# The first pair's decay: a one-hot product on TensorE in place of a fetch from DRAM

## The chip, the cores and the metric

The kernel runs on one core of a Trainium2 chip. The metric is the device time of one execution in microseconds; the median of several executions is compared.

## What is computed

Attention with a cumulative decay over 4 batches, 8 heads, 576 positions and head size 64, then two gated layers over the 2304 tokens, all in 32-bit floats:

```
cum = cumsum(log(clip(f, 1e-4, 1)), axis=-1)             # [4, 8, 576]
scores = q @ k.T / sqrt(64) + cum[..., :, None] - cum[..., None, :]   # causal
attn = softmax(scores)
x = (attn @ v) as [2304, 512]
x = (sigmoid(x @ w_gate) * (x @ w_val)) @ w_out           # 512 -> 1536 -> 512
h = x @ w_in2
out = (h * clip(h + 3, 0, 6) / 6) @ w_out2                # 512 -> 2048 -> 512
```

In a row of scores `cum` at the query's own position is the same for every key, so the softmax needs only the term of the keys. The kernel keeps the scores negated and adds `cum` of the key.

## The kernel before

The attention works through 16 pairs of heads (class `Pair`, from line 293). For a pair the queries and keys of its two heads are loaded by SP (`load`, line 308; the values by `load_v`, line 314), turned by TensorE and copied to `qp` and `kp`, with a small piece for the last 64 queries in `qz` (`prep`, line 334). Then come four units of scores (`scores`, line 371): s=1 holds the first 256 queries, s=2 and s=3 the next two blocks of 128 (384 and 512 keys wide), and s=4 the last 64 queries of both heads together. For each unit VectorE adds the decay to the scores and takes the minimum of each row (`expo`, `least`, line 410), ScalarE (ACT in the profile) does the exponential with its sum, VectorE the reciprocal, GpSimd (POOL) the scaling (`norm`, line 456), TensorE turns the result (`flip`, tile `tt`), ScalarE copies it out, and TensorE multiplies it with the values (`values`, tile `pv`). SP issues nearly all loads and stores.

The decay that `least` reads is the tile `dc`: `cum` of the pair's two heads, 2 x 576 numbers, the same in all 128 partitions. At the start `cumulate` (line 268) loads f with (batch, head) on 32 partitions, clips it on VectorE, takes the logarithm on ScalarE, forms the running sum `cum` with one scan on VectorE and stores it to the DRAM tile `cum_d`. For each pair `load_decay` (line 317) fetches two rows of `cum_d` back, each spread over 128 partitions by the transfer. `tail_decay` (line 323) makes from `dc` a masked copy `dt` for s=4, on POOL. The pool of `dc` has two buffers, that of `dt` one.

The first pair is set up ahead of the loop, lines 1134 to 1140, and there stands `warm_up` too (line 1091): 24 products (`WU`) of a zero tile `z`, in bf16, 512 columns wide, whose results in the PSUM tiles `o` nobody reads. They write to the pool `psF` with two buffers, which later serves the products of the gated layer. The three-buffer pool `psB` holds the turned tiles `tq`, `tk`, `tl` and `tt`.

In the attention the order of the instructions on each engine is set by a scheduler, from its own estimate of times, except where `keep_in_program_order` binds TensorE's products. From the second layer on (line 1240) it is the order of the program. Between the attention's products TensorE gets pieces of the first gated layer (`Filler`), and VectorE, ScalarE and POOL convert that layer's weights (`single`, line 104; tile `raw`).

Of the kernel before, what the change touches and what calls it, by code (L numbers as in the profile page):

```python
# [7 lines left out]
F32 = mybir.dt.float32  # L8
# [4 lines left out]
ALU = mybir.AluOpType  # L13
# [7 lines left out]
def attn_moe_kernel(  # L21
# [13 lines left out]
    nc = tc.nc  # L35
    B, H, S, D = q.shape
# [3 lines left out]
    P = 128  # L40
# [3 lines left out]
    TAIL = S - NQ * P  # L44
# [15 lines left out]
    def split_sbuf(hi, lo, src, eng_hi, eng_lo):  # L60
# [10 lines left out]
        out=ident, in_=ident, compare_op=ALU.not_equal, fill=1.0, base=0,  # L71
        pattern=[[-1, P]], channel_multiplier=1,
# [6 lines left out]
    for d in (masks[:, :P], mask):  # L79
        nc.gpsimd.affine_select(  # L80
            out=d, in_=d, compare_op=ALU.is_ge, fill=BIG, base=0,
            pattern=[[-1, P]], channel_multiplier=1,
# [145 lines left out]
    pe = Tensor()  # L228
# [4 lines left out]
    a2 = att.enter_context(tc.tile_pool(name="a2", bufs=2))  # L233
# [3 lines left out]
    ep = att.enter_context(tc.tile_pool(name="ep", bufs=7))  # L237
    sm = att.enter_context(tc.tile_pool(name="sm", bufs=10))
    psA = att.enter_context(tc.tile_pool(name="psA", bufs=NA, space=PSUM))
    psB = att.enter_context(tc.tile_pool(name="psB", bufs=6 - NA, space=PSUM))  # L240
# [27 lines left out]
    def cumulate():  # L268

        fl = ax.tile([P, S], F32, tag="x0", name="fl")[: B * H]  # L270
        ones = ax.tile([P, S], F32, tag="x0", name="ones")[: B * H]
        cum = ep.tile([P, S], F32, tag="e", name="cum")[: B * H]
        nc.scalar.dma_start(fl, f.rearrange("b h s -> (b h) s"))
        nc.vector.memset(ones, 1.0)
        nc.vector.tensor_scalar(fl, fl, 1.0e-4, 1.0, ALU.max, ALU.min)
        nc.scalar.activation(fl, fl, AF.Ln)
        nc.vector.tensor_tensor_scan(cum, ones, fl, 0.0, ALU.mult, ALU.add)
        nc.scalar.dma_start(cum_d, cum)

    def load_nat(t, src, b, hp, last):  # L280

        for j in range(2):
            nc.sync.dma_start(
                t[:, :NQ, j, :], src[b, 2 * hp + j, : NQ * P, :].rearrange("(c p) d -> p c d", p=P)
            )
        for p0, x in last:
            nc.sync.dma_start(
                t[p0 : p0 + TAIL, NQ, :, :],
                x[b, 2 * hp : 2 * hp + 2, NQ * P : S, :].rearrange("h p d -> p h d"),
            )  # L290
        return t

    class Pair:
# [23 lines left out]
        def load_decay(self):  # L317
            h0 = self.b * H + 2 * self.hp
            self.dc = a2.tile([P, 2, S], F32, tag="dc", name="dc")
            both = cum_d[h0 : h0 + 2].rearrange("h s -> (h s)").rearrange("(o x) -> o x", o=1)  # L320
            nc.sync.dma_start(self.dc.rearrange("p h s -> p (h s)"), both.to_broadcast([P, 2 * S]))

        def tail_decay(self):


            self.dt = a1.tile([P, S], F32, tag="dt", name="dt")
            for j in range(2):
                r = slice(64 * j, 64 * j + 64)
                nc.gpsimd.affine_select(
                    out=self.dt[r], in_=self.dc[r, j], compare_op=ALU.is_ge, fill=BIG, base=NQ * P,  # L330
                    pattern=[[-1, S]], channel_multiplier=1,
                )
# [585 lines left out]
    class Second:  # L918
# [93 lines left out]
        def unit(self, k, x, ys, temps, between={}):  # L1012
            u1, u2, p5 = temps
            g, tt = self.ga[k % 2], nc.vector.tensor_tensor
            r11, r22, r12 = self.act(u1, g, 0, 0), self.act(p5, g, 1, 1), self.act(u2, g, 1, 0)
            r21 = self.act(x(), g, 0, 1)
            then = {1: (r11,), 2: (r11,), 3: (r11,), 4: (r22,), 5: (r12, r22, r22), 6: (r21, r12, r12, r21, r21)}
            for s in range(7):
                if s in (1, 3):
                    y = ys.pop(0)()  # L1020
                o = y if s % 2 else x()
                self.product(o, k, s, s in (0, 1, 3))
                if s in (0, 2, 3):
                    nc.scalar.copy({0: u1, 2: u2, 3: p5}[s], o)  # L1024
                elif s < 6:
                    c = {1: u1, 4: p5, 5: u2}[s]
                    tt(c, c, o, ALU.add)  # L1027
                for r in then.get(s, ()):
                    next(r)
                if k % NQ2 == NQ2 - 1:  # L1030
                    self.load_block(k // NQ2 * 7 + 7 + s)
                if s in between:
                    between[s]()
# [57 lines left out]
    def warm_up(n):  # L1091
        z = ep.tile([P, S], F32, tag="e", name="z").bitcast(BF16)[:, :512]
        nc.gpsimd.memset(z, 0.0)
        for _ in range(n):
            o = psF.tile([P, 512], F32, tag="F", name="o")
            nc.tensor.matmul(o, z[:, :P], z, start=True, stop=True)
# [6 lines left out]
    EA = (nc.scalar, nc.gpsimd, nc.gpsimd)  # L1103
    EF = (nc.scalar, nc.scalar, nc.gpsimd)
    WU = 24

    KD, TL = 4, 3

# [10 lines left out]
    psF = fa.enter_context(tc.tile_pool(name="psF", bufs=2, space=PSUM, side="right"))  # L1119
# [8 lines left out]
    fill = Filler(wa, NCA)  # L1128
    pairs = [
        Pair(i, i // NP, i % NP, list(range(1, NQ + 1) if i < UP else range(NQ, 0, -1)))  # L1130
        for i in range(B * NP)
    ]
    units = [(p, s) for p in pairs for s in p.order]
    cumulate()
    pairs[0].load()
    pairs[0].load_decay()
    pairs[0].load_v()
    pairs[0].tail_decay()
    warm_up(WU)
    pairs[0].prep()  # L1140
# [63 lines left out]
    for t in range(len(units) + 3):  # L1204
        for job in (scores, values, expo, flip, norm, some, prep):
            job(t)
        p, s = unit(t - 3)
        if p and s == p.order[-1] and p.hp == NP - 1 and p.b < NCA:
            done = p.b + 1
        p, s = unit(t - 5)  # L1210
# [71 lines left out]
```

## Time and profile before

| | us |
|---|---|
| three runs | 1030.00, 1032.05, 1037.42 |
| median | 1032.05 |
| profiled execution | 1031.56 |
| its span, first to last instruction | 1029.8 |

The profile shows one execution. Its engines are PE (TensorE's products) and PEld (TensorE's loads of the stationary operand), DVE (VectorE), ACT (ScalarE), POOL (GpSimd) and SP (the queue that issues DMAs, SPq). L215 is the helper through which the products go, L219 that of the transposes, so tiles tell them apart. A row of the timeline gives start, duration, engine, line, operation, output <- inputs, number of instructions and in brackets the idle time of the engine before it with what ended it. An f32 product that is not a transpose has two records for each instruction of the order, and consecutive ones overlap: what one costs the next is seen in the distance of their starts.

### The profile page before, as it was taken

The page shows a single profiled execution, that of the slowest core. Times are in us where ns is not written, and L with a number is a line of the kernel's source. Part 1 is how long each engine was busy: PE and PEld are TensorE (multiplying, and loading weights), DVE is VectorE, ACT ScalarE, POOL GpSimd, SP SyncE. Part 2 cuts the span into 40 slices and gives each one's busy share as a digit, 9 for nine tenths or more (in the row PEclk, how much of TensorE's full clock was granted, in tenths as well). Part 3 has the DMA queues.
Part 4 walks back from the last instruction along what each step waited for, and adds up shares of the span by engine and source line. Part 5 has one row for each costly group of instructions (what it writes and reads, how often), then busy time and mean ns, then how long its engine had stood idle before and what let it go on. Part 6 is the DMA issues. An engine that isn't in the chain of part 4 may idle for free.

```text
span 1029.8 us, 15579 instructions
## 1 busy us (share of the span) xinstructions
PE 1015.4 (99%) x5410; PEld 835.2 (81%) x5410; DVE 530.3 (51%) x1206; ACT 466.0 (45%) x1052; POOL 304.4 (30%) x385
## 2 busy tenths in 40 slices
PE   7999999999999999999999999999999999999998
PEld 4667766776778888998888888898988988989987
DVE  5687755536435654447568567444434444233222
ACT  5776466456554442323334434434434434334332
POOL 3576755445333322120324323111111111111110
PEclk9999999999999999999999999999999999999999
DMA  7987567355232435284696758766495755744211
GB/s 196 259 252 215 163 197 197 115 163 169 82 132 87 139 122 165 75 283 176 248 341 247 236 174 317 250 250 219 147 362 191 279 208 189 286 170 174 75 72 62
DMA packets 120911, 197.79 MB, mean 192 GB/s; under 512 B 63936, under 2 KB 73152, under 8 KB 116736
## 3 DMA queue, kind: packets, MB, share of 16 engines
q1 hardware_dynamic: 120736, 196.64, 57.0%
q8 instruction: 43, 0.70, 0.3%
q14 instruction: 36, 0.29, 0.1%
q10 hardware_dynamic: 96, 0.15, 0.0%
HBM read 143.47 MB, written 53.29 MB: 191 GB/s over the span
## 4 chain that ended last, share of the span: by engine, by line
PE 93%; DMA 2%; DVE 2%; ACT 1%; issue 1%; POOL 1%; SPq 0%; POOLq 0%; ACTq 0%; DVEq 0%
PE po L215 33%; PE pv L215 19%; PE u L215 17%; PE pg L215 15%; PE st L215 5%; PE tt L219 3%; DMA x_d<-x 1%; DMA big<-x_d 1%; PE tq L219 1%; PE tk L219 1%; DMA dc<-cum_d 0%; DVE e L411 0%; ACT e L419 0%; POOL e L456 0%; DVE raw L108 0%
## 5 line engine op out<-in xcount | busy, mean ns | idle before, releaser
L215 PE MATMUL po<-w,big 128*128 128x512 f32 x864 | 200.5, 390 | 0.0
L215 PEld LDWEIGHTS po<-w,big 128*128 128x128 f32 x864 | 161.9, 188 | 32.8
L215 PE MATMUL pg<-big,wg 128*128 128x512 f32 (+1 forms) x720 | 166.7, 373 | 2.6 <-DMA big<-x_d 2.6
L215 PE MATMUL pv<-big,wv 128*128 128x512 f32 (+1 forms) x720 | 166.7, 373 | 0.0
L215 PE MATMUL po<-big,wo 128*128 128x512 f32 (+1 forms) x720 | 164.4, 372 | 0.1
L215 PEld LDWEIGHTS po<-big,wo 128*128 128x128 f32 x720 | 124.9, 189 | 27.4 <-issue 2.9
L215 PEld LDWEIGHTS pg<-big,wg 128*128 128x128 f32 x720 | 124.2, 189 | 28.3 <-DMA big<-x_d 4.4
L215 PEld LDWEIGHTS pv<-big,wv 128*128 128x128 f32 x720 | 124.9, 189 | 24.7 <-issue 3.1
L1027 DVE TENSOR_TENSOR h<-h,u 128x384 f32<-128x384 f32 x69 | 38.2, 554 | 155.2 <-PE u L215 155.2
L456 POOL TENSOR_SCALAR e<-e,m 128x256 f32<-128x256 f32 (+4 forms) x144 | 85.2, 606 | 57.4 <-DVE m L454 35.1
L419 ACT ACTIVATE e<-e,m 128x256 f32<-128x256 f32 (+4 forms) x144 | 83.8, 584 | 39.2 <-DVE m L411 35.8
L215 PE MATMUL u<-h,big 128*128 128x384 f32 x504 | 90.6, 336 | 0.4 <-DVE h L1027 0.4
L215 PE MATMUL u<-h,h 128*128 128x384 f32 x504 | 90.2, 336 | 0.0
L215 PEld LDWEIGHTS u<-h,big 128*128 128x128 f32 x504 | 88.2, 188 | 2.1 <-DVE h L1027 1.1
L215 PEld LDWEIGHTS u<-h,h 128*128 128x128 f32 x504 | 88.4, 188 | 1.0
L976 POOL TENSOR_TENSOR big<-tail,big 128x384 fp32r<-128x384 f32 x30 | 30.8, 1027 | 196.3 <-PE u L215 115.7
L1024 ACT COPY h<-u 128x384 f32<-128x384 f32 x69 | 32.6, 473 | 112.9 <-PE u L215 112.9
L111 ACT ACTIVATE raw<-raw 128x512 f32<-128x512 f32 x68 | 45.5, 681 | 66.5 <-DVE raw L108 65.3
L739 DVE SCALAR_TENSOR_TENSOR sg<-sg,pv 128x512 f32<-128x512 f32 (+1 forms) x48 | 29.6, 618 | 82.8 <-PE pv L215 64.8
L411 DVE CUSTOM_DVE_ANT_0 e<-st,dc 128x384 f32<-128x384 f32 (+3 forms) x110 | 53.5, 519 | 32.5 <-PE st L215 27.1
L114 DVE SCALAR_TENSOR_TENSOR raw<-raw 128x512 int32<-128x512 int32 x68 | 52.1, 775 | 14.6 <-ACT raw L111 14.2
L219 PE MATMUL tt<-ident,e 128*128 128x128 f32 x384 | 55.8, 276 | 1.2 <-POOL e L456 1.2
(135 smaller groups left out, 1247.3 us busy)
## 6 DMA issues: line engine op xcount, KB each, us to landing
h<-xc_d SPq DMA_DIRECT2D x21, 768.0 KB, 6.8
big<-x_d SPq DMA_DIRECT2D x56, 256.0 KB, 3.6
raw<-in_moe_w_out_dram SPq DMA_DIRECT2D x28, 512.0 KB, 3.8
h<-wt_d SPq DMA_DIRECT2D x12, 1024.0 KB, 7.0
big<-wt_d SPq DMA_DIRECT2D x12, 1024.0 KB, 7.3
dc<-cum_d SPq DMA_DIRECT2D x16, 576.0 KB, 4.7
x_d<-x SPq DMA_DIRECT2D x32, 288.0 KB, 3.5
h<-wb_d SPq DMA_DIRECT2D x12, 768.0 KB, 4.5
```

The costliest lines, as they stand in the source:

```text
L111: nc.scalar.activation(e, e, AF.Copy, scale=2.0**-112)
L114: nc.vector.scalar_tensor_tensor(low, high, 3, low, ALU.logical_shift_left, ALU.bitwise_or)
L215: i = nc.tensor.matmul(*a, **k)
L219: i = nc.tensor.transpose(*a)
L411: i = nc.vector.tensor_tensor_reduce(out=e, in0=st, in1=d, op0=ALU.add, op1=ALU.min, scale=1.0, scalar=init, accum_out=m[:, a : a + 1],)
L419: nc.scalar.activation(e, e, AF.Exp, bias=m[:, a : a + 1], scale=-1.0, accum_out=m[:, 4 + b : 5 + b])
L456: nc.gpsimd.tensor_scalar(e, e, m[:, 12 + j : 13 + j], 1.0, ALU.mult, ALU.mult)
L739: pace["dve"] = nc.vector.scalar_tensor_tensor(sg, sg, 1.0, pv, ALU.add, ALU.mult)
L976: (nc.vector if f else nc.gpsimd).tensor_tensor(lo, sg, hi.bitcast(F32), ALU.subtract)
L1024: nc.scalar.copy({0: u1, 2: u2, 3: p5}[s], o)
L1027: tt(c, c, o, ALU.add)
```

## The change

`load_decay` is no longer called for the first pair. In its place `spread_decay` makes on POOL a tile `pick` of 32 partitions and 2 x 128 columns, which holds ones in the row of the first or of the second head and zeros elsewhere. Three pairs of f32 products on TensorE, each with `pick` of one head as the stationary and a stretch of `cum` as the moving operand (256, 64 and 256 columns), give `cum` of the head in all 128 partitions. ScalarE copies the first 256 and the last 64 columns of both heads from PSUM to `dc`, VectorE the middle 256. The first and the last stretch use `psF`, the tail `psB`. The store to `cum_d` stays, and all other pairs fetch as before.

```diff
@@ cumulate
         nc.scalar.dma_start(cum_d, cum)
+        return cum
@@ class Pair
+        def spread_decay(self, cum):
+
+            h0 = self.b * H + 2 * self.hp
+            pick = ep.tile([P, S], F32, tag="e", name="pick")[: B * H, : 2 * P].rearrange("p (j c) -> p j c", j=2)
+            nc.gpsimd.memset(pick, 0.0)
+            nc.gpsimd.affine_select(
+                out=pick, in_=pick, compare_op=ALU.not_equal, fill=1.0, base=-h0,
+                pattern=[[-1, 2], [0, P]], channel_multiplier=1,
+            )
+            self.dc = a2.tile([P, 2, S], F32, tag="dc", name="dc")
+            for c0, n, copy, pool, tag in (
+                (0, 2 * P, CO[0], psF, "F"), (4 * P, TAIL, CO[1], psB, "B"), (2 * P, 2 * P, CO[2], psF, "F")
+            ):
+                o = pool.tile([P, 512], F32, tag=tag, name="pd")[:, : 2 * n].rearrange("p (j c) -> p j c", j=2)
+                for j in range(2):
+                    pe.matmul(o[:, j], pick[:, j], cum[:, c0 : c0 + n], start=True, stop=True)
+                copy(self.dc[:, :, c0 : c0 + n], o)
@@
     WU = 24
+    CO = (nc.scalar.copy, nc.scalar.copy, nc.vector.tensor_copy)
@@
-    cumulate()
+    cum = cumulate()
     pairs[0].load()
-    pairs[0].load_decay()
     pairs[0].load_v()
+    pairs[0].spread_decay(cum)
     pairs[0].tail_decay()
     warm_up(WU)
```

The scheduler then puts the instructions of the first three pairs in another order; behind them every engine's order is the one before. On TensorE the start of the program was this (`identb` and `masks` for the causal mask, `qn` and `kn` the loaded q and k, `z` the warm-up):

```order
L215 MATMUL st<-masks,identb 128x384
L219 MATMUL tq<-ident,qn 128x128 x4
L1096 LDWEIGHTS z
L1096 MATMUL o<-z 128x512
L1096 LDWEIGHTS z
L1096 MATMUL o<-z 128x512
L219 MATMUL tk<-ident,kn 128x128 x4
```

and now, with `pd` the products with the one-hot tile, it is this:

```order
L215 MATMUL st<-masks,identb 128x384
L215 MATMUL pd<-cum,pick 128x256 x2
L215 MATMUL pd<-cum,pick 128x64 x2
L215 MATMUL pd<-cum,pick 128x256 x2
L219 MATMUL tq<-ident,qn 128x128 x4
L219 MATMUL tk<-ident,kn 128x128 x4
L1115 LDWEIGHTS z
L1115 MATMUL o<-z 128x512
L219 MATMUL tl<-ident,kn 128x128
```

The six products stand ahead of the first transposes, and no warm-up product stands ahead of either.

Further on, while the second pair's scores are made, TensorE's order before (tt_422 is the first turned tile of the first pair's s=3, tt_427 the second, tt_450 that of s=4; st_437 to st_485 are scores of the second pair) was:

```order
L1096 LDWEIGHTS z_192
L1096 MATMUL o_240<-z_192 128x512
L219 MATMUL tt_422<-ident_74,e_338 128x128 x4
L215 MATMUL st_437<-kp_313,qp_312 128x384
L215 MATMUL st_438<-kp_313,qp_312 128x384
...
L219 MATMUL tt_427<-ident_74,e_339 128x128 x4
L219 MATMUL tt_450<-ident_74,e_364 128x128 x4
```

and at the same place now (tt_438, tt_443 and tt_466 are the same three tiles):

```order
L219 MATMUL tt_438<-ident_74,e_354 128x128 x4
L1115 LDWEIGHTS z_208
L1115 MATMUL o_242<-z_208 128x512
L215 MATMUL st_453<-kp_329,qp_328 128x384
L215 MATMUL st_454<-kp_329,qp_328 128x384
...
L1115 LDWEIGHTS z_208
L1115 MATMUL o_244<-z_208 128x512
L219 MATMUL tt_443<-ident_74,e_355 128x128 x4
L1115 LDWEIGHTS z_208
L1115 MATMUL o_246<-z_208 128x512
L219 MATMUL tt_466<-ident_74,e_380 128x128 x4
```

The 24th warm-up product stood ahead of tt_422; now the 16th does, and eight follow, up to the values of the first pair.

On VectorE the order between the scan and the first score operation, which order prints as ISA, is now this:

```order
L277 SCALAR_TENSOR_TENSOR cum<-ones,fl 32x576
L340 COPY dc<-pd 128x2x256
L363 TENSOR_SCALAR qp<-tq 128x512
L368 COPY kp<-tk 128x512
L376 TENSOR_SCALAR qz_144<-tl 64x64 x2
L363 TENSOR_SCALAR qp<-tq 128x512
L430 ISA e,m<-st,dc 128x128
```

Before, it was the same without the copy. On SP the first pair's fetch of `dc` is gone; the third pair's, which stood between the loads of the fourth pair's k, now stands behind three loads of weights (`raw`) and right ahead of the fourth pair's own.

## Rows read from the trace of the kernel before

**Rows 1.** Page, busy us of each engine, share of the span, instructions.

```profile
PE 1015.4 (99%) x5410; PEld 835.2 (81%) x5410; DVE 530.3 (51%) x1206; ACT 466.0 (45%) x1052; POOL 304.4 (30%) x385
```

**Rows 2.** Windows: busy time by engine in each stretch, then granted clock, DMA share.

```profile
core 0: us, PE busy (x) PEld busy (x) DVE busy (x) ACT busy (x) POOL busy (x), PEclk, DMA share, GB/s
0.00:23.00 23.00, 17.65 (x93) 9.73 (x94) 12.92 (x50) 11.17 (x30) 8.97 (x25) 1.00 0.76 185
23.00:50.00 27.00, 26.84 (x185) 17.02 (x185) 17.92 (x73) 19.68 (x62) 13.84 (x24) 1.00 0.93 264
50.00:75.00 25.00, 23.84 (x165) 14.39 (x161) 20.27 (x67) 19.84 (x58) 19.34 (x27) 1.00 0.83 243
...
310.00:650.00 340.00, 340.00 (x1708) 290.56 (x1707) 201.52 (x313) 130.31 (x226) 89.53 (x68) 1.00 0.59 203
```

**Rows 3.** The chain that ended last, from its start: start us, us, what.

```profile
0.72 2.58 DMA fl<-in_f_dram
...
5.91 2.00 DMA cum_d<-cum
...
7.92 5.09 DMA dc<-cum_d
...
22.64 0.66 PE tt L219 x4
23.30 1.06 PE st L215 x6
```

**Rows 4.** Timeline of PE, 0 to 26 us.

```profile
4.29 1.09 PE L219 MATMUL tq<-ident,qn 128*128 128x128 f32 x4 [0.90 <-DMA qn<-in_q_dram]
5.17 1.06 PE L1096 MATMUL o<-z 128*128 128x512 bf16 x2
6.02 1.06 PE L219 MATMUL tk<-ident,kn 128*128 128x128 f32 x4
6.88 0.63 PE L1096 MATMUL o<-z 128*128 128x512 bf16 x1
...
10.21 0.63 PE L219 MATMUL tq<-ident,qn 128*128 128x128 f32 x4 [0.27 <-DMA qn<-in_q_dram]
10.68 1.90 PE L1096 MATMUL o<-z 128*128 128x512 bf16 x8
...
17.72 0.65 PE L215 MATMUL st<-kp,qz 128*128 128x288 f32 x2
18.21 0.59 PE L1096 MATMUL o<-z 128*128 128x512 bf16 x2
```

**Rows 5.** Timeline of all engines, 5 to 14 us: VectorE's operations and ACT's table load.

```profile
5.80 0.65 DVE L344 TENSOR_SCALAR qp<-tq 128x512 f32<-128x512 f32 x1
...
7.12 0.69 DVE L349 COPY kp<-tk 128x512 f32<-128x512 f32 x1 [0.67 <-PE tk L219]
...
7.99 1.28 ACT L419 ACT_TABLE_LOAD   x1
8.00 0.46 DVE L357 TENSOR_SCALAR qz<-tl 64x64 f32<-64x64 f32 x2 [0.19 <-ACT kp L354]
...
10.88 0.69 DVE L344 TENSOR_SCALAR qp<-tq 128x512 f32<-128x512 f32 x1 [2.41 <-PE tq L219]
...
13.03 0.29 DVE L411 CUSTOM_DVE_ANT_0 e<-st,dc 128x128 f32<-128x128 f32 x1 [1.47 <-DMA dc<-cum_d]
```

**Rows 6.** Waits of 22.6 to 31.3 us: waited for, us in total, times, longest.

```profile
DVE e L411 <- PE st L215: 2.1, 2, 1.1
```

**Rows 7.** Windows, the same stretch; columns as in the rows 2.

```profile
22.60:31.30 8.70, 8.66 (x65) 5.41 (x65) 6.04 (x27) 6.51 (x22) 4.31 (x9) 1.00 0.91 258
```

**Rows 8.** Timeline of SP and POOL, 28 to 33 us, and dc's transfer issued there.

```profile
28.18 0.41 SPq L321 DMA_DIRECT2D dc<-cum_d  x1
...
32.80 1.39 POOL L329 TENSOR_SCALAR_AFFINE_SELECT dt<-dc 64x576 f32<-64x576 f32 x2 [0.30 <-DVE m L411]
...
DMA to landing us min/median/max: 8.1/8.1/8.1
```

## The prediction

> **What bounds the kernel now.** I read the page's busy shares first: TensorE is busy for 1015.4 us of the 1029.8 us span [rows 1]. What is left is not spread evenly, and the windows show where it lies: the first 23 us hold 5.35 us of TensorE's idle time (23.00 - 17.65), the next 27 us hold 0.16 us, and from 310 to 650 us there is none [rows 2]. So two things set the time: when TensorE's queue fills up for good, and how much work it then holds. Next comes the chain that ended last, read from its start [rows 3]. It begins with the load of f, goes through clamp, logarithm and scan, whose result stands at 5.9 us, and then spends 2.00 us on the store to DRAM and 5.09 us on the fetch. VectorE's first score operation starts at 13.03 us, having waited 1.47 us for that fetch [rows 5]. From 22.64 us on the chain is TensorE, piece after piece.
>
> The profiled execution took 1031.56 us, 1.76 us more than its span and 0.49 us less than the median of 1032.05; the three runs reach from 1030.00 to 1037.42. My sum is made against 1031.56.
>
> **What goes.** The 7.1 us of store and fetch leave the chain. The store itself stays, since the other pairs need it, and one fetch of 576 KB less runs among the early loads. This does not buy 7.1 us. VectorE had nothing else to do only for the last 1.47 us: before that it stood in order behind the second pair's qp copy, which began at 10.88 and took 0.69 [rows 5]. If the decay were there at no cost and nothing else moved, the first score operation could start 1.47 us earlier, and that is the whole prize.
>
> **What comes: six products on TensorE, ahead of the transposes.** They wait for the scan, so they start at about 5.9 us, and the first transposes, which ran from 4.29 us before, now stand behind them. Their price: an f32 product over 288 columns, which is two passes and so two records, started at 17.72 and the next product at 18.21 [rows 4]; a pass takes 0.245 us, or 0.85 ns a column. The six have 1,152 columns, or 2,304 in two passes: 1.96 us. Early in this trace TensorE is slower than that. Two warm-up products take the 0.85 us from 5.17 to 6.02, 0.425 us each; eight of them from 10.68 take 1.90 us together, some 0.21 each [rows 4]. [...] At the early spacing, twice as long, the six take 3.9 us. Bounds: 2.0 and 3.9.
>
> [...]
>
> I take 3.9: TensorE began its transposes at 4.29 us before and still ran at the wide spacing up to 6.02 [rows 4]; now it starts 1.6 us later. So the products end at 9.8 us, and their last value is out 0.2 us after (the lone warm-up product at 6.88 lasts 0.63, against the spacing of 0.425 [rows 4]): 10.0 us.
>
> **Behind them, VectorE in order.** The order puts five VectorE operations between the products and the first score: the copy of the last third (128x512, as the kp copy, 0.69), qp 0.65, kp 0.69, the two qz pieces 0.46, and the second pair's qp 0.69 [rows 5]. That is 3.18 us, and the first score operation starts at 13.2 us, against 13.03. The transposes fit under it: after 9.8 us eight of them take 1.7 us even at the wide spacing of 0.215 each [rows 4], and qp needs only the first four. Two ACT copies lie beside the products. The load of the exp table (1.28 us [rows 5]) now starts behind the copy of kp's tail, at 11.3 to 12.4 us, and so ends at 12.6 to 13.7; the first exponential is due at about 13.5, so at worst it costs 0.2, which I leave out. POOL's two operations for the one-hot tile follow its memsets and end long before the scan does. So the start is +0.2 us late: the fetch's 7.1 us are given back to products and copies in front of the same operation. The bounds: at the fast spacing products end at 7.9 and VectorE's row would allow 11.3, but the second pair's q, for which TensorE waited until 10.21 [rows 4], holds its qp until about 11.6, so -1.4; if TensorE stays slow through the transposes, 13.9, so +0.9.
>
> **What moves: the warm-up products.** 24 stand in the program as before. Before, all had been issued when TensorE came to the first transposes of the 128x512 scores, at 22.64 us. Now eight of them stand behind that place, one or two between each group of transposes, scores and values. There they are not free: from 22.60 to 31.30 TensorE is busy for 8.66 of 8.70 us [rows 7], and VectorE waits there for TensorE's scores, 2.1 us in all, not the other way round [rows 6]. Eight at 0.216 (the spacing of the row of eight: 1.90 less the last one's 0.39, over seven) make 1.7 us. Bounds: nothing, if waits that only this order has leave room for them, and 1.7. I take 1.7, since the only rows of this place show no room.
>
> **SyncE.** With one fetch and its wait of 0.5 us gone, all loads behind go out about 1 us earlier; nothing waits for them in this stretch. One is put back: the third pair's decay, sent before at 22.2 us, now stands behind three weight loads, next to the fourth pair's. Its wait is met when the first pair's last score operation has read the buffer. POOL takes it at 32.80 us [rows 8]. I reckon it sent at 23 to 27 us, landed after 5 to 8 us, and not late: nothing.
>
> **Sum.** 1031.56 + 0.2 + 1.7 = 1033.5 us. A shift at 31 us goes through to the end: behind it the instructions stand in the order they had, and TensorE idles 1.2 us between 50 and 75 us and not at all from 310 to 650 [rows 2].
>
> **Rivals.**
> 1. *Faster: the products run at the fast spacing and the warm-up products fall in gaps.* The first score then starts at 11.6 us, 1.4 us early: 1031.56 - 1.4 = 1030.2. For it: the granted clock reads 1.00 throughout. Against it: the 0.425 us spacing, and the full TensorE behind 22.6 us. It decides if the last third is copied before about 9 us.
> 2. *The two terms cancel.* Either the fast products' 1.4 us pay for the eight (1031.56 - 1.4 + 1.7 = 1031.9), or the products are slow and the eight fit in gaps (1031.56 + 0.2 = 1031.8). For it: each bound by itself is possible; against: the same rows as above.
> 3. *Slower: the third pair's decay lands late.* The fetch sent at 28.18 us, behind the same three weight loads, took 8.1 us to land [rows 8]. Sent at 26.7 us it would land at 34.8, 2.0 us after POOL wanted it at 32.80; POOL's queue holds the scaling of the next probabilities behind that mask, and TensorE's transposes wait for those. With the slow start's 0.9: 1031.56 + 0.9 + 1.7 + 2.0 = 1036.2. It decides if the fetch lands after the place where POOL is ready for it. Against it: the loads run earlier, so it should be sent well ahead of that.
>
> **How the numbers follow.** Forecast 0.45, rival 1 0.15, rival 2 0.2, rival 3 0.2. The predicted time is the forecast's 1033.5. The range takes in all four, and stops a little outside their ends, at 1030.0 and 1036.6, for the spread of runs and what I can't see. A measurement of this kernel tells about 1%, 10 us, from no change. None of the cases comes near that: the whole prize is 1.47 us and the dearest rival costs 4.6. So within 1% has 0.93; 0.03 is left for faster and 0.04 for slower, for mechanisms that no row shows.
>
> **What would show it.** Right: in the profile after, the six products fill TensorE from 5.9 us to near 10; the first score operation on VectorE starts at 13.0 to 13.4 us and waits for VectorE's own queue, not for a DMA; from 22 to 32 us warm-up products stand among busy TensorE work and the second pair's values end about 1.9 us later than before. Wrong: a first score before 12 us; TensorE idle in front of the late warm-up products; or POOL waiting for the decay's DMA near 33 us. A gain or loss of more than 5 us would say that the order behind the start does more than carry a shift through.

## Result and the profile after

| | us |
|---|---|
| this kernel, median of 14 runs | 1037.65 (1035.54 to 1040.23) |
| kernel before, median of 14 runs beside it | 1031.64 (1030.00 to 1037.42) |
| ratio | 1.0053, 95% interval 1.0042 to 1.0064 |
| profiled execution after | 1040.23, span 1038.5 |

The change costs about half a per cent, 6.0 us by the medians. That is within 1%, as forecast, but it lies above the range. The profiled execution is the slowest of the 14; a second one (1035.24 us, below) is used beside it.

The page's busy row after, to be read against [rows 1]:

```profile
PE 1021.7 (98%) x5422; PEld 841.2 (81%) x5422; DVE 530.8 (51%) x1207; ACT 468.0 (45%) x1054; POOL 305.3 (29%) x387
```

TensorE is busy 6.3 us more and idle 2.4 us more (1038.5 - 1021.7 = 16.8 against 14.4). The chain that ended last begins like this after the change (start us, us, what), against [rows 3]:

```profile
4.70 1.36 DVE cum L277
...
6.19 4.60 PE pd L215 x12
10.79 1.05 PE tq L219 x4
11.84 0.85 PE tk L219 x4
...
13.75 0.53 PE tq L219 x4
...
14.50 0.91 PE st L215 x8
15.41 0.27 DVE e L430
```

From the scan to the first score operation everything is TensorE: the products, then the transposes with warm-up products between them, then the scores. VectorE's rows say the same; its operations wait for TensorE one after the other, and the first score operation starts at 15.39 us, not at 13.03 [rows 5]:

```profile
10.83 0.69 DVE L340 COPY dc<-pd 128x512 f32<-128x512 f32 x1 [4.78 <-PE pd L215]
11.87 0.69 DVE L363 TENSOR_SCALAR qp<-tq 128x512 f32<-128x512 f32 x1 [0.35 <-PE tq L219]
12.72 0.69 DVE L368 COPY kp<-tk 128x512 f32<-128x512 f32 x1 [0.16 <-PE tk L219]
...
14.33 0.69 DVE L363 TENSOR_SCALAR qp<-tq 128x512 f32<-128x512 f32 x1 [0.26 <-PE tq L219]
15.39 0.29 DVE L430 CUSTOM_DVE_ANT_0 e<-st,dc 128x128 f32<-128x128 f32 x1 [0.37 <-PE st L215]
```

Windows after (columns as in [rows 2]); the first three answer to [rows 2, 7]:

```profile
0.00:23.00 23.00, 17.26 (x81) 11.32 (x82) 12.67 (x41) 9.89 (x26) 7.19 (x23) 1.00 0.74 173
23.00:50.00 27.00, 26.93 (x186) 16.55 (x184) 16.27 (x69) 18.66 (x58) 13.74 (x24) 1.00 0.78 227
22.60:31.30 8.70, 8.70 (x54) 5.03 (x52) 4.28 (x23) 6.70 (x22) 5.30 (x10) 1.00 0.89 282
...
170.00:175.00 5.00, 4.45 (x20) 3.00 (x18) 1.63 (x5) 2.35 (x4) 2.17 (x4) 0.66 0.34 86
250.00:255.00 5.00, 3.54 (x13) 2.68 (x14) 3.06 (x11) 2.90 (x9) 2.60 (x6) 0.78 0.30 84
255.00:260.00 5.00, 5.00 (x39) 2.97 (x39) 2.98 (x12) 3.86 (x13) 2.79 (x4) 0.88 0.08 20
```

In the first 23 us TensorE idles 5.74 us, hardly more than the 5.35 before. So the 4.60 us of products did not go into its waits; they stand in front of its work. The last three rows are new: here the granted clock is 0.66, 0.78 and 0.88. The trace's list of granted clocks has 0.50 from 170.83 and from 252.75 us, 3.41 us each time, and 1.00 between them and behind, up to 1037.82. Before, it was 1.00 in the same stretches:

```profile
170.00:175.00 5.00, 5.00 (x33) 3.73 (x30) 2.78 (x6) 1.70 (x5) 3.28 (x6) 1.00 0.85 223
250.00:255.00 5.00, 5.00 (x28) 3.73 (x29) 2.88 (x5) 1.37 (x3) 2.89 (x5) 1.00 0.86 255
```

What the clock lost is 5 x 0.34 = 1.7 us in the first place and 5 x (0.22 + 0.12) = 1.7 us in the second.

Ahead of both places TensorE waits. Its timeline after (the first row, sixteen products of the gated layer, is a mark that stood at 140.85 us before):

```profile
144.51 3.95 PE L215 MATMUL po<-big,wo 128*128 128x512 f32 x16
...
169.12 0.73 PE L215 MATMUL pg<-big,wg 128*128 128x512 f32 x2 [1.85 <-DMA big<-x_d]
169.69 0.60 PE L219 MATMUL tq<-ident,qn 128*128 128x128 f32 x4
170.84 2.08 PE L215 MATMUL pg<-big,wg 128*128 128x512 f32 x4 [0.55 <-DMA big<-x_d]
...
251.40 0.73 PE L215 MATMUL pg<-big,wg 128*128 128x512 f32 x2 [2.26 <-DMA big<-x_d]
```

At the turn from one batch to the next the attention's x is stored to DRAM (`x_d<-x`) and loaded again (`big<-x_d`) for the gated products. Before, the waits for it were 0.80 and 1.41 us (and 0.35 a little later). The same rows before:

```profile
140.85 3.95 PE L215 MATMUL po<-big,wo 128*128 128x512 f32 x16
...
164.41 0.73 PE L215 MATMUL pg<-big,wg 128*128 128x512 f32 x2 [0.80 <-DMA big<-x_d]
...
243.46 0.73 PE L215 MATMUL pg<-big,wg 128*128 128x512 f32 x2 [1.41 <-DMA big<-x_d]
```

The shift was 3.66 us at the mark and still so at 163 us, 7.10 behind the first reload, 9.20 behind the second and 8.7 at the end. Of the two steps, 3.44 and 2.10 us, the longer waits make 1.60 and 0.50 (1.85 + 0.55 - 0.80; 2.26 - 1.41 - 0.35); the rest, 1.8 and 1.6, agrees with the two falls of the clock. So the loss has two parts: one from the start, one from the two reloads.

### The profile page after: what moved, and what is told of

Read it like the earlier page. It is cut to its first block, busy times and chain, and to the rows that moved or that the text cites. A ratio compares the mean times of both kernels' runs of the same rounds, so it can differ in the third digit from the quotient of the medians.

```text
span 1038.5 us, 15608 instructions
## 1 busy us (share of the span) xinstructions
PE 1021.7 (98%) x5422; PEld 841.2 (81%) x5422; DVE 530.8 (51%) x1207; ACT 468.0 (45%) x1054; POOL 305.3 (29%) x387
## 4 chain that ended last, share of the span: by engine, by line
PE 94%; DVE 2%; DMA 2%; ACT 1%; issue 1%; POOL 0%; SPq 0%; POOLq 0%; ACTq 0%; DVEq 0%
PE po L215 33%; PE pv L215 18%; PE u L215 17%; PE pg L215 15%; PE st L215 6%; PE tt L219 3%; DMA x_d<-x 1%; PE tk L219 1%; PE tq L219 1%; DMA big<-x_d 1%; PE pd L215 0%; PE o L1115 0%; DVE e L430 0%; ACT e L438 0%; DVE raw L108 0%
```

## Experiments

They are numbered as their labels. In all of them the kernel before ran beside on the same chip; its medians were 1029.9 to 1031.1 us. A "mark" is the first of the sixteen products above, at 140.85 us in the profile before and 144.51 after.

**1 and 2: are the late warm-up products dear?** The changed kernel with 16 and with none:

```diff
-    WU = 24
+    WU = 16        # second: WU = 0
```

> The changed kernel with 16 warm-up products in place of 24: TensorE's order is the same but for the last eight, which are gone. Theory A (the late start and the eight warm-up products among busy work make the loss): the eight stand in the chain that ended last between 26 and 33 us, so it takes 8 x 0.216 = 1.7 us less than the changed kernel's 1037.65, about 1035.9, and the third pair's first 128x384 scores come 1.7 us earlier than 39.66 us. Rival B (the eight lie in gaps, the loss is made at the start and in later DMA waits): no less than 1037.2. Rival C (the loss is made by the waits on the reload of x near 165 and 250 us): no change in the place of the third pair, and a time that follows those waits.

> The changed kernel without any warm-up product. Theory A: the chain between 18.8 and 33 us holds some 15 of them, so up to 3.2 us less than 1037.65, about 1034.5, if TensorE still comes to its fast spacing as early as it does now (14 us). Rival (the warm-up products are what brings the fast spacing early): transposes and scores stay at twice the spacing beyond 14 us, the first score starts no earlier than 15.4 us, and the time is 1037 or more.

With 16: 1037.77 us, ratio 1.0067 (1.0046 to 1.0088); first score 15.32, mark 144.26. Taking away the eight late ones moved the mark by 0.25 us and the time not at all. Its chain shows what takes their place, a wait for VectorE:

```profile
27.15 0.46 PE tt L219 x4
27.60 0.41 issue
28.02 0.56 DVE e L430
```

The reading by which they cost 0.216 us each falls; they lie in gaps that this order has. With none: 1034.39 us, 1.0037 (1.0023 to 1.005); first score 14.94, mark 144.31. The mark did not move, yet 3.4 us went. In the profiles the difference lies behind the mark: with 16 the wait near 245 us was 2.58 us with a clock of 0.74 behind it, with none 1.31 us and no fall.

**3: the kernel before without warm-up.**

```diff
-    WU = 24
+    WU = 0
```

> The kernel before without any warm-up product, decay fetched as before. Theory A: the first score waits for the fetch at 13.0 us whatever TensorE does, and the warm-up products lay in waits, so 1031 to 1032, as before. Rival (they bring the fast spacing early and their loss costs): 1033 or more, with twice the spacing beyond 13 us.

1031.64 us, 1.0007 (0.9995 to 1.0019); first score 13.38. TensorE kept the wide spacing until 19 us (0.21 us a transpose from 15.86, 0.11 from 19.01) and the mark stood at 143.66, 2.8 us late, but the time hardly suffered: the waits for the reloads were 0.23 and 1.48 us.

**4: transposes ahead of the products, no warm-up.**

```diff
+    pairs[0].prep()
     pairs[0].spread_decay(cum)
     pairs[0].tail_decay()
-    warm_up(WU)
-    pairs[0].prep()
```

> The changed kernel with the first pair's transposes written ahead of the one-hot products, and no warm-up product. On TensorE the turned q and k come first, then the products. Theory A: the transposes run while the scan does, the products run from about 6.1 to 10.7 us at the wide spacing, and behind them only small copies are left, so the first score starts at 12.5 to 13.5 us, against 15.4; with no warm-up product in the chain the time is 1031 to 1033. Rival (the store and the late DMAs make the loss, not the start): 1036 or more though the first score is early.

1032.45 us, 1.0025 (1.0014 to 1.0035); products 3.71 and 1.04 us, first score 13.41, mark 143.53, waits 0.20 and 0.93. Two microseconds less than with none in the changed order: standing ahead of the transposes is what made the first score late.

**5: the changed kernel again, unaltered.**

> The changed kernel once more, unaltered, for a second profile of it. Theory (the start is late by 2.4 us for good, and on top the length of a store and reload of x varies from execution to execution; where TensorE waits about 2 us or more for one, its granted clock falls and the stretch behind costs 1.5 to 2 us more): first score 15.3 to 15.5 and +3.5 to +3.7 us at 141 us as in the first profile, but the waits for the reload at 165 and 250 us come out different from 1.85 and 2.26 us, and the executions with a mean clock of 0.999 to 1.0 lie within 1035 to 1037, those at 0.996 to 0.998 within 1037 to 1040. Rival (the new program makes these waits long by its order): both waits again within 0.3 us of 1.85 and 2.26, and the clock below 0.7 behind the first.

1036.08 us, 1.0059 (1.0037 to 1.0082). In its profiled execution (1035.24 us) the first score started at 15.83, the waits for the reloads were 0.87 and 2.02 us, and the clock stayed at 1.00. So neither reading held in full: the first wait is chance from run to run, the second came back long. Of all 18 executions ten had a mean clock of 0.998 or less, of 124 of the kernel before, in all these experiments, only 26; there the median of those 26 is 1032.9, of the others 1030.3.

**6: late without any product.** The kernel before with the scan written three times:

```diff
         nc.vector.tensor_tensor_scan(cum, ones, fl, 0.0, ALU.mult, ALU.add)
+        nc.vector.tensor_tensor_scan(cum, ones, fl, 0.0, ALU.mult, ALU.add)
+        nc.vector.tensor_tensor_scan(cum, ones, fl, 0.0, ALU.mult, ALU.add)
```

> The kernel before with the scan of the decay written three times instead of once: the fetch of the first pair's decay, and so the first score, starts two scans later (2 x 1.34 us by the row of the scan), and no product and none of the changed order is in it. Theory (lateness of the first score is what costs, whatever made it late): first score near 15.7, +3.0 to +4.0 us at the pair-2 outputs that stood at 140.92, median 1033 to 1037, with falls of the granted clock in more executions than the kernel before has. Rival (the products and the order on TensorE cost by themselves, a late decay is taken up by slack): +1.5 us or less at 140.92, median below 1032.5.

1033.28 us, 1.002 (1.0008 to 1.0032), between the two readings. VectorE's row:

```profile
15.74 0.29 DVE L413 CUSTOM_DVE_ANT_0 e<-st,dc 128x128 f32<-128x128 f32 x1 [2.12 <-DMA dc<-cum_d]
```

As late as in the changed kernel, and it costs 2.8 us by the medians, half of the loss. The mark stood at 143.24, 1.3 to 1.7 us earlier than in the two profiles of the changed kernel: in those TensorE spent the time ahead of the first score on the products, in run 6 it did transposes and warm-up products while it waited. The profile, the slowest of its ten executions, also has a wait of 2.04 us for the reload near 169 us with a fall of the clock behind it. So such falls come without any product, too.

**7 and 8: products behind transposes and warm-up products.** The changed kernel, its start rewritten (7: four and eight warm-up products; 8: five and eleven; only the lines that set the order of 7 are shown):

```diff
-    pairs[0].spread_decay(cum)
-    pairs[0].tail_decay()
-    warm_up(WU)
-    pairs[0].prep()
+    z = warm_tile()
+    warm_up(z, 4, psF.tile([P, 512], F32, tag="F", name="o"))
+    pairs[0].prep()
+    pairs[0].spread_decay(cum)
+    pairs[0].tail_decay()
+    warm_up(z, 8)
```

> The changed kernel with its start in another order: four warm-up products between the first pair's transposes, all transposes ahead of the six products, eight warm-up products written last. Theory (the products cost 3.9 to 4.6 us because TensorE runs them at the wide spacing, and the transposes behind them carry that on; ahead of them and warmed up they cost near 2 us): six products in 2.0 to 2.6 us, ending by 10.7, first score 11.3 to 12.7, less than +0.5 us at 140.92 against the kernel before, median 1028.5 to 1031.0. Rival (the products do not get faster with a warmed TensorE: K of 32 rows and f32 set their time): products 3.7 us or more, first score 13.3 or later, median 1032 to 1034.5.

> As the run before it, with five warm-up products between the transposes and eleven written last, which fill TensorE's gaps between 11 and 30 us. If warm-up products behind the first scores are what keeps the narrow spacing until 30 us, this is 0.3 to 1.0 us faster than the variant with four and eight; if they only fill gaps, the two lie within 0.4 us of each other; if they delay work in a full stretch, it is slower by 0.22 us for each of the three more.

The seventh: 1030.71 us, 1.0001 (0.9991 to 1.001), no difference from the kernel before. Its chain:

```profile
4.34 1.09 PE tq L219 x4
5.43 1.71 PE o L1118 x4
7.14 0.85 PE tk L219 x4
7.99 0.21 PE tl L219
8.21 2.73 PE pd L215 x12
10.94 0.91 PE st L215 x8
...
11.95 0.29 DVE e L430
...
19.10 0.37 SPq L284
19.51 2.15 DMA kn<-in_k_dram
```

The products take 2.73 us and the first score starts at 11.95, 1.1 us before that of the kernel before. The mark is at 140.90 all the same: behind the start the chain goes over VectorE, ScalarE and a load of keys, so the gain is waited away before the mark. The eighth: 1035.37 us, 1.0042 (1.0027 to 1.0057), 4.7 us slower, with a first score at 12.28 and a mark at 141.25. None of the three expectations covers that; lateness is 0.4 us. Its wait near 245 us is 2.29 us, with a clock of 0.69 behind it, where the seventh waited 1.46 with none: 0.8 us of wait and 1.7 of clock. The profile is of its fastest execution, 1032.84; what made the others slower still is not shown.

**What lies on the reload.** The page lists queue q8 with 43 packets of together 0.70 MB, in the kernel before and after, under the kind "instruction": 16 KB each. Their places go with TensorE's records more evenly than with those of VectorE or POOL: windows from the start of one packet to the next hold 92 to 147 PE records before the change and 93 to 150 after, of VectorE 10 to 53 and 8 to 62, of POOL 0 to 29 and 0 to 31. With its weight loads TensorE has 2 x 5,422 records after the change, by estimate some 250 to a packet (10,844 over 43). No trace shows what a packet holds or whose it is; the kind and these counts led me to the reading that the place of a packet goes by how many TensorE instructions have gone before, and that a packet on a reload makes the reload longer. The expectations from here on call this the theory of the packet, or of the instruction packet. A reload comes in two halves of 256 KB, each with an issue of its own. The table has where the packets stand in nineteen profiles; the length is that of the half in the chain, from issue to landing:

| reload of x | profiles | its length, us |
|---|---|---|
| near 245 us, a q8 packet under way between its issue and its landing | 8 (after; runs 1, 5, 8, 10, 13, 16, 18) | 3.05 to 3.85 |
| near 245 us, the packet behind its landing | 11 (before; runs 2, 3, 4, 6, 7, 9, 12, 14, 15, 17) | 2.51 to 2.71 |
| near 165 us, a packet inside | 8 (before; runs 1, 5, 6, 7, 8, 12, 13) | 3.34 to 4.76 |
| near 165 us, in its last 0.5 us or behind | 10 (runs 2, 3, 4, 9, 10, 14 to 18) | 2.81 to 3.10 |

In the first profile after, the packet near 165 us fell on the store instead, which took 5.53 us (2.39 to 3.10 in the others).

Near 245 us TensorE's count tells the two apart in all nineteen: 5,414 or 5,422 PE records on the page where the packet is on the reload, 5,386 to 5,410 where it comes behind. Near 165 us it does not. Over all halves issued from 150 to 262 us the median length is 3.48 us with a packet wholly inside (44 halves) and 2.70 with none (127). It is not so each time: in run 10 the first half near 245 us took 2.66 us with the packet inside it, and there, as in the first profile after, it was SP's issue of the second half that came out long (0.58 and 1.03 us against 0.32).

**9: twelve warm-up products**, the order of the run with 16 on every engine, eight instructions fewer:

```diff
-    WU = 24
+    WU = 12
```

> The changed kernel with twelve warm-up products instead of twenty-four: the same order as the run with sixteen on every engine, four warm-up products (eight TensorE instructions) fewer. [...] Rival (the long waits come from the late start or by chance): as with sixteen, wait 1.9 us or more, clock fall, median 1037 to 1038.5; four warm-up products fewer in gaps are worth at most 0.3.

By the theory of the packet I expected it behind the reload near 245 us, a wait of 0.9 to 1.5 us there and a median of 1034 to 1036. It came to 1033.72 us, 1.0027 (1.0016 to 1.0038), a little below the range expected and 4 us less than with 16 (on another chip), one execution of twelve at a clock of 0.998 or less. The start is late as before: first score 15.94, mark 143.99. The wait near 245 us is 1.36 us, and no clock falls in the profile.

**10 and 11: eight instructions with hardly any work**, added to run 7 and to the kernel before, the order the same on every engine:

```diff
+    for _ in range(4):
+        nc.tensor.matmul(o[:, :4], z[:, :P], z[:, :4], start=True, stop=True)
```

> The run with four warm-up products between the transposes, to which four products of 128x128 by 128x4 are added behind those four, eight TensorE instructions more, the order the same on every engine. Theory of the instruction packet: it falls into the reload near 245 us, whose wait grows from 1.46 to 2.0 to 2.6 us, the granted clock falls behind it in many executions, median 1032 to 1035.5 against 1030.7. Rival (work and lateness alone count): at most 0.3 us for the four small products, median 1030.5 to 1031.3.

> The kernel before with four products of 128x128 by 128x4 written behind the warm-up products, eight TensorE instructions more, the order the same on every engine. Theory of the instruction packet: first score and outputs near 141 us stand where they did (within 0.4 us), the packet near 245 us falls into the reload, its wait grows from 1.41 to 2.0 to 2.6 us with a fall of the granted clock in many executions, median 1031.5 to 1035. Rival: at most 0.3 us, median 1030.2 to 1031.0.

Run 10: 1033.40 us, 1.0026 (1.0011 to 1.0041), with a wide spread, 1030.24 to 1036.92. The packet came inside, wait 2.30 us, clock 0.77. But the profile has a second cause, in its chain:

```profile
8.35 4.56 PE pd L215 x12
12.91 1.58 PE st L215 x8
```

The products ran at the wide spacing here, 4.56 us against 2.73, behind the same work but for the four small products. So it doesn't tell the packet's price alone. Run 11: 1032.35 us over eleven executions, 1.0004 (0.9992 to 1.0016); the twelfth, the one that was profiled, took 1686 us and is left out, so the kernel was run again (16).

**12: run 7 without the eight last warm-up products.**

```diff
-    warm_up(z, 8)
```

> The run with four warm-up products between the transposes, without the eight that were written last: 16 TensorE instructions fewer. By the theory of the instruction packet it comes behind the reload near 245 us and perhaps behind the one near 165 us too (waits 0.2 to 0.5 there instead of 1.6): 0.5 to 1.5 us off the second wait. Against it: without warm-up products behind the first scores TensorE may go back to the wide spacing between 11 and 20 us, as in the kernel before without any, which cost 2.8 us at 141 us. Median 1029.0 to 1030.5 if the spacing holds, 1031 to 1033 if it does not.

1032.99 us, 1.0017 (1.0002 to 1.0032), from 1029.77 to 1038.63. In the profile the products took 2.37 us, first score 11.36, mark 140.78; both of the waits were there, 0.46 and 0.92 near 165 with a packet inside, 1.88 near 245 behind a store of 4.08 us. So the packet did not come behind the reload near 165 us, and the median is above the 1029.0 to 1030.5 expected at the narrow spacing. The spread is as wide as that of run 10; that some executions get the narrow spacing by the products and some don't would explain both, but each has only one profile.

**13: run 9 with four small products**, as many instructions as with 16; **16: run 11 again.**

> The changed kernel with twelve warm-up products, to the first of which four products of 128x128 by 128x4 are added, order the same on every engine as with twelve alone: as many TensorE instructions as with sixteen, and 0.1 to 0.3 us of work. Theory (the place of the instruction packet decides): packet within 2 us behind the issue of the reload near 245 us, wait there 1.9 us or more, clock falls in half of the executions or more, median 1036 to 1038.5, as with sixteen. Rival (the amount of warm-up work decides): as with twelve, wait 1.3 to 1.5 us, median 1033.5 to 1034.3.

> The kernel before with four products of 128x128 by 128x4 behind the warm-up products, once more, for its profile. Theory of the packet: wait for the reload near 245 us of 1.9 us or more, packet inside that reload, first score within 0.4 us of 13.03. Rival: wait 1.0 to 1.5 us, packet behind the reload as in the kernel before.

Run 13: 1035.58 us, 1.0042 (1.0029 to 1.0055). Its chain near 245 us:

```profile
241.32 3.57 DMA x_d<-x
...
244.90 3.71 DMA big<-x_d
...
248.65 0.73 PE pg L215 x2
```

and that of run 9 at the same place:

```profile
239.88 3.47 DMA x_d<-x
...
243.37 2.71 DMA big<-x_d
...
246.12 0.73 PE pg L215 x2
```

The DMA view of run 13, of the reload's own stretch (queue: packets, MB, share of 16 engines; issue: KB, us to landing):

```profile
q8 instruction: 1, 0.02, 2.2%
...
big<-x_d SPq DMA_DIRECT2D x2, 256.0 KB, 3.7
```

The same view of run 9 has no row of q8:

```profile
q1 hardware_dynamic: 551, 0.54, 66.8%
...
big<-x_d SPq DMA_DIRECT2D x2, 256.0 KB, 2.8
```

The one packet takes 2.2% of 16 engines for 3.71 us, which is 1.3 us on one of them; the reload is 1.0 us longer, and the wait grows from 1.36 to 2.45 us. The median, on another chip than run 9's, lies between the two readings, and two of the five executions had a mean clock of 0.998 or less, fewer than expected. Run 16: 1032.57 us, 1.0015 (1.0005 to 1.0025). The packet was inside the reload (3.05 us), but the waits were 0.88 and 0.75, not 1.9: this profile misses what was expected of it. The executions as a whole do differ: of runs 11 and 16 together 13 of 21 had a mean clock of 0.998 or less, against 26 of 124 of the kernel before.

**14 and 15: fewer instructions, to beat both kernels.** The kernel before with twelve warm-up products; and the start of run 7 with six, none later, and the products merged:

```diff
-    WU = 24
+    WU = 12
```

```diff
-            for c0, n, copy, pool, tag in (
...
+            for j in range(2):
+                w = psF.tile([P, 512], F32, tag="F", name="pd")
+                pe.matmul(w, pick[:, j], cum[:, : 4 * P], start=True, stop=True)
+                CO[2 * j](self.dc[:, j, : 4 * P], w)
```

> The kernel before with twelve warm-up products instead of twenty-four, 24 TensorE instructions fewer. By the theory the packet near 165 us comes behind the reload, as in the three runs with 24 instructions or fewer ahead (waits 0.20 to 0.25 instead of 0.80 us), and the one near 245 us stays behind it: 0.3 to 0.9 us faster than before and fewer falls of the clock, median 1029.3 to 1030.5, if the twelve that are left keep the narrow spacing until the first scores. If TensorE returns to the wide spacing between 13 and 20 us, 1031 to 1032.5, as without any.

> The changed kernel with six warm-up products between the first pair's transposes, all transposes ahead, and the one-hot products merged to four (two of 512 columns, two of 64): 28 TensorE instructions of warm-up and products ahead instead of 72. Six warm-up products to make the narrow spacing come by the products in every execution. If it does: products 2.0 to 2.7 us, first score 11.8 to 12.6, both packets behind the reloads (waits 0.2 and 0.9 to 1.5 us), median 1028.5 to 1030.0, below the kernel before. If the packet near 165 us still falls on the reload: 0.7 more. If the spacing stays wide: first score 14.5 or later, median 1032 to 1034.

Run 14: 1030.10 us, 0.9996 (0.9987 to 1.0005); waits 0.30 and 1.08, lowest profile of all (span 1027.7), but no difference that can be told. Run 15: 1031.06 us, 1.0006 (0.9995 to 1.0017); products 2.43 us, first score 12.35, waits 0.18 and 1.25, and still from 1029.08 to 1034.36. Nothing here beats the kernel before for certain.

**17 and 18: runs 9 and 13 side by side on one chip.**

> The changed kernel with twelve warm-up products, beside the next run on the same chip. Theory of the packet: it comes behind both reloads (waits below 0.5 us near 165 us and 0.9 to 1.5 near 245), median 2.2 to 3.2 us above the kernel before. Rival: the same here; the two part on the next run.

> The same with the four products of 128x4 added, on the same chip. Theory of the packet: inside both reloads, which last 3.0 us or more where the other's last 2.6 to 3.0; 1.5 to 3 us slower than with twelve alone. Rival (work decides): 0.0 to 0.3 us slower.

1035.92 us, 1.0049 (1.0034 to 1.0064), and 1036.29 us, 1.0056 (1.0044 to 1.0068). The reloads are as the packet would have them, 2.81 and 2.66 us in the one, 2.83 and 3.48 with the packet in the other, and so are the waits near 245 us, 1.59 and 2.69. Near 165 us the packet came behind the reload in both, not inside it in the second as expected. The medians don't follow: they are 0.4 us apart, next to the rival's bound. In the first kernel's profile the clock fell at a place where no reload is:

```profile
65.00:70.00 5.00, 4.02 (x19) 1.98 (x19) 4.20 (x12) 4.87 (x16) 2.75 (x4) 0.92 0.69 190
70.00:75.00 5.00, 5.00 (x16) 2.19 (x17) 2.31 (x8) 1.83 (x5) 3.74 (x7) 0.50 0.77 237
75.00:80.00 5.00, 5.00 (x39) 3.33 (x37) 4.05 (x12) 2.34 (x6) 3.03 (x4) 0.89 0.80 232
```

TensorE idled 0.98 us there, waiting for POOL and VectorE, and lost 5 x (0.08 + 0.50 + 0.11) = 3.5 us. Of the six executions three had full clock, median 1033.7; the other kernel's two had 1035.6. So the packet's effect on the reload near 245 us is shown; what it costs in the median is 0.4 to 2 us by these two pairs (the first on two chips) and stays open, as falls elsewhere cover it.

## Why the prediction was wrong

**The start: +0.2 forecast, 2.4 at the first score and 3.7 at the mark.** "At the early spacing, twice as long, the six take 3.9 us" came out as 4.60, and they began at 6.19, not 5.9. So VectorE's copy behind them starts at 10.83 instead of 10.0, which is 0.8 of the 2.2 us that the forecast of 13.2 missed. The step that failed is the next one, and it holds the other 1.4: "The transposes fit under it". I reckoned only VectorE's five operations behind the products and let the transposes run beside them. In the trace VectorE waits for each of them (0.35, 0.16 and 0.26 us idle ahead of its three copies, then 0.37 ahead of the score), because they stand behind the products in TensorE's queue, at the wide spacing, with warm-up products in between: tq, tk, tl, the second tq and eight score records from 10.79 to 15.41. My upper bound, 13.9, was too low for the same reason. Runs 4 and 7 show it from the other side: with the transposes ahead the first score starts at 13.41, and at 11.95 with products of 2.73 us.

I also took the start for a matter of the first score alone. It isn't: run 6 is as late and stands 1.3 to 1.7 us better at the mark. The store and fetch that the change removed were hidden waits in which TensorE did transposes and warm-up; the products are 4.6 us of work on the engine that bounds the kernel.

**The clock: the spacing was the right thing to go by, but it stayed wide for longer than I read.** The forecast went by the spacing and not by the granted-clock column, which reads 1.00 at the start before and after. The list of granted clocks in the traces says why. Its first entry, full clock, begins at 8.38 us before and at 13.82 after (1.00 in both), and there the distance of TensorE's transposes falls from 0.21 to 0.11 us; ahead of it nothing is recorded, and the column counts that as 1.00. So the wide spacing lasted not to 6.02 us, as I read from [rows 4], but to 8.38, and the change made it last 5.4 us longer, over all of the products and most of the transposes. Products of 4.56 and 2.73 us behind nearly the same work (runs 10 and 7) bear that out: the entry begins at 16.80 in the one and at 8.92 in the other. The two profiles of the changed kernel differ in it too, 13.82 and 14.72 us, and I had given no term to that.

Both things cost, as the marks show. Where the entry begins by 9.2 us and the first score by 13.1 (before; runs 7, 8, 12, 14 to 16), the mark stands at 140.51 to 141.25. In run 6 only the first score is late: 143.24. In runs 3 and 4 the wide spacing lasts to 18.65 and 16.87 us while the first score starts near 13.4: 143.66 and 143.53. In all the others both are late: 143.91 to 144.94, but for run 17 with its fall ahead of the mark (147.06).

**The warm-up products: +1.7 forecast, 0.25 measured** for the eight at the mark. "The only rows of this place show no room" was true of the order before. In the new order the stretch is as full (8.70 of 8.70 us) because the warm-up products fill it: without the eight, in run 1, TensorE waits for VectorE there (8.20 of 8.70 us busy). A full row in one order is no proof for another; the bound "nothing, if waits that only this order has leave room" was the right one.

**"A shift at 31 us goes through to the end": failed.** It held from 50 to 163 us, and behind 260 us the shift stayed between 9.2 and 8.5. Between them lie two places at which TensorE waits for a store and a reload, and the new number of TensorE instructions puts a q8 packet on the reload near 245 us, where the kernel before has it behind. With the packet there the reload is 0.3 to 1.3 us longer, and the wait is 2.0 to 2.7 us in seven of eight profiles, instead of 0.9 to 1.9. The granted clock falls behind five of these eight waits, at 1.7 us each, and behind none of the other eleven. By the medians this and what else lies behind the mark is 6.0 - 3.7 = 2.3 us. The trace of the kernel before had these waits (2.6 us of idle time between 155 and 260 us), and I passed over them because the change touches nothing there.

**The rivals.** The third pair's decay did not land late: POOL's mask of that pair follows its work without idle time. Neither did the products run fast, nor did the terms cancel. The prediction's own warning came true: more than 5 us means that the order behind the start does more than carry a shift through.

**What stays open.** Of the 6.0 us, the start is shown in place (3.7 us at the mark), and so are the longer reloads and the falls. How the 3.7 us divide between the late score and the wide spacing is not shown: either alone gives 2.4 to 2.8 (runs 6, 3 and 4). How often the clock falls, why it fell at 69 us in run 17, and why the narrow spacing comes at 8.92 us in run 7 and not before 16.80 in run 10, behind the same four warm-up products, was not found.

## What to carry to other kernels

Before work takes the place of a DMA round trip, ask whether the engine that gets it is waiting at that moment. Here TensorE had transposes to do: ahead of these the products took 4.60 us and the mark came 3.7 us late; behind them and four warm-up products, in run 7, they took 2.73 us and the mark was where it had been (140.90 against 140.85). So put such work behind what that engine could do meanwhile, and ask at which spacing it will run. A full stretch of the bounding engine says nothing about the same stretch in another order (8.70 of 8.70 us busy with the eight late warm-up products, 8.20 without). Where an engine waits for a store and reload with little to spare, even the number of instructions ahead of it can move that wait, as near 245 us here (1.36 us in run 9, 2.45 in run 13 with eight more): look at the small queues of the DMA list, here q8, before blaming the work that the change adds.

## What was not expected of the hardware

- With a 16 KB packet of q8 on it, a 256 KB half of the reload near 245 us took 3.05 to 3.85 us instead of 2.51 to 2.71 (eight profiles against eleven).
- Eight TensorE instructions of next to no work (four products of 128x4) moved that packet by 4.0 us against the reload, from behind it to inside (runs 9 and 13: 5.1 and 1.1 us after the issue of its first half; 17 and 18: 4.6 and 0.6). In between TensorE waits for the reload (in run 9 for 1.36 us, up to 246.12) and starts no product, which fits so long a way.
- At the start TensorE's operations take twice their later distance (transposes 0.21 us against 0.11, before and after) while the column of the granted clock reads 1.00: it counts a stretch without a record as full clock. The first record begins between 7.66 us (run 12) and 18.65 us (run 3).
- A fall of the granted clock costs 1.7 us (3.41 us at 0.50 in the first profile after), the same in seven places behind a wait for a reload (the first profile after at 170 and at 250 us, runs 1, 6, 8, 10 and 18). In run 17 it cost 3.5 us, behind waits of 0.73 and 0.25. In run 15 it fell at 12.32 us, to 0.73 in the window from 10 to 15 us, although TensorE had not waited since 4.27.
